# Delta rule and feed-forward on one core: the key products as 112-column products, the Gram products as 32-column ones

## The chip, the cores and the metric

The kernel runs on one core of a Trainium2 chip. The metric is the time of one execution on the device in microseconds (us). A run of a kernel is timed several times, and its median counts. One more execution is recorded instruction by instruction by the hardware profiler; all rows below come from that one.

The core has a matrix engine (PE, whose weight loads are listed apart as PEld), a vector engine (DVE), a scalar engine (ACT), GpSimd (POOL), and queues that start DMAs (SP here). Each engine works through its own instructions in a fixed order; an instruction whose input is late holds up everything behind it on that engine.

## The reference

Per head, a state of 48 x 48 is carried over 768 tokens. There are 4 x 8 = 32 heads. What the attention gives goes through two dense layers with a softplus between them.

```python
for t in range(S):
    kt, vt, bt = (k_n[:, :, t], v[:, :, t], beta[:, :, t, None])     # k_n: k over its norm
    y[:, :, t] = np.einsum('bhd,bhde->bhe', q[:, :, t], state)
    v_old = np.einsum('bhde,bhd->bhe', state, kt)
    state = state + bt[:, :, :, None] * np.einsum('bhd,bhe->bhde', kt, vt - v_old)
...
h = x @ w_in                                      # 3072 x 384 by 384 x 2048
g = np.maximum(h, 0.0) + np.log1p(np.exp(-np.abs(h)))
return (g @ w_out).astype(np.float32)
```

## The kernel before, in words

**Chunks.** The 768 tokens are cut into 12 chunks of 64 (`NS`, `C`). Within a chunk s the recurrence is solved with matrices: the Gram product K K^T of the chunk's keys (`gram`, L127) gives a triangular system, which is inverted (`invert`, on DVE, for two chunks at a time); `k_state` (L295) forms K S with the state S and takes it from the scaled values in `NV` (L299); `u_all` (L319) multiplies the inverse with them to U; `p_half` (L305) forms P, the products of keys and queries, and `mask_p` (L312) copies P under a triangular mask into the array `big`; `y_all` (L346) forms the outputs from the state, P and U; `state` (L331) makes the next state.

**Layout.** Heads go in 16 pairs, a head of a pair in each half of the 128 partitions. `big` has for each head 112 columns (`QW`): 64 for the queries or the masked P, then 48 for the state or U. `bv` and `be` are views of it, `be` sorted by the parity e of the pair. `tk[h]`, `dr[h]`, `lo[h]`, `hi[h]` are partition ranges: 64 tokens, the 48 feature rows in the opposite half, and the lower and upper 32 tokens. A product of 64 rows and 64 still columns occupies one quarter of PE's array, given by the half of its rows and the half of its output partitions. `quads` lists the 32 products of a step so that four neighbours take four different quarters; `k_state`, `gram` and `u_all` go by it. `p_half` uses two of the quarters only: rows in `dr[ab]`, outputs in `tk[ab]`. All these products are in fp32, and the trace has two matmul rows for each.

**Buffers.** Results of PE go to PSUM. The attention has four buffers there (`ps_a`, tile name `pa`), taken in turn; the dense layers have two for the first (`ps_h`, `ph`) and one for the second (`ps_o`, `po`). A product that needs a buffer waits until what stood in it has been read.

**What empties the Gram product.** ACT, in 12 copies per chunk: 8 of 32 partitions (L132) take the diagonal 32 x 32 blocks to `work`, 4 (L118) take the blocks below them to `off`.

**The dense layers** (`moe`) run beside the attention, chunk by chunk: L466 makes the hidden values, L470 to L472 on ACT and L474 to L477 on DVE make the softplus (and split it into a rounded part and a rest), L449 multiplies by the second weights. In the first chunk the weights are converted as well (L385 to L420).

**Order.** Up to the first chunk's state the order on PE, DVE, ACT and POOL is the order of the code (`manual_schedule`). From there on, generators for attention and dense layers yield pieces which `attend` and `target` mix, and the framework then settles the order of each engine when the program is built, with its own picture of time. PE works through pieces of both layers; the last tenth of the run is dense layers alone.

Chunks with an even number begin with `begin`: `cross_a` (L264), `arrange` and `cross_b` (L285, its result copied by ACT at L288) complete the inverses of two chunks. Even chunks 2, 4, 6 and 8 end with the Gram products of the two chunks after the next (`gram(s + 2)`, `gram(s + 3)`). The code of a chunk, around the change:

```python
k_state(s)
mask_p(0, p_half(s, 0))
yield
u_all(s)
...
mask_p(1, p_half(s, 1))
```

Of the kernel before, what the change touches and what calls it, by code (L numbers as in the profile page):

```python
# [7 lines left out]
F32 = mybir.dt.float32  # L8
# [4 lines left out]
ALU = mybir.AluOpType  # L13
# [4 lines left out]
B, H, S, D = 4, 8, 768, 48  # L18
NT, DM, DFF = B * S, H * D, 2048
P = 128  # L20
C = 64
HB = 32
# [13 lines left out]
def deltanet_moe(ctx, tc, kT, qT, kN, kI, vN, beta, wts, out):  # L36
# [33 lines left out]
    maskP = const.tile([P, C], F32, name="maskP")  # L70
    half = const.tile([P, 1], F32, name="half")
    bet = const.tile([P, NS, NP], F32, name="bet")
    W, HF, ST, OFF, TT, LTD, LDS, NN, NV, X = {}, {}, {}, {}, {}, {}, {}, {}, {}, {}

    copies = (nc.scalar.copy, nc.vector.tensor_copy)

# [25 lines left out]
    def parity(t):  # L102
        return t.rearrange("p (a e) c -> p e a c", e=2)
# [16 lines left out]
    def gram(s):  # L120
        if s not in OFF:
            OFF[s] = two.tile([P, NP, HB], F32, name="off", bufs=3)
        pas = [ps_a.tile([P, NP // 2, C], F32, name="pa") for e in range(2)]
        kt = kts[s % 3]
        for i, e, p, ab, t in quads:
            k = kt[dr[ab], p, :]
            nc.tensor.matmul(pas[e][tk[t], i, :], k, k, start=True, stop=True)  # L127
        u, j = divmod(s, 2)
        for e in range(2):
            for h in range(2):  # L130
                for rows, c in ((lo[h], 0), (hi[h], HB)):
                    nc.scalar.copy(parity(LTD[u][rows, j * NP:(j + 1) * NP])[:, e],  # L132
                                   pas[e][rows, :, c:c + HB])
        copy_below(s, pas)

    def gram_diagonal(s, pool, name):
        pas = [pool.tile([P, NP // 2, HB], F32, name=name) for e in range(2)]
# [150 lines left out]
            copies[s < 1 and h](tt[lo[h], :, HB:], pm[lo[h]])  # L288


    def k_state(s):

        pks = [ps_a.tile([P, NP // 2, D], F32, name="pa") for e in range(2)]
        for i, e, p, ab, t in quads:
            nc.tensor.matmul(pks[e][tk[t], i, :], kts[s % 3][dr[ab], p, :], bv[dr[ab], ab, p, C:],  # L295
                             start=True, stop=True)
        for e in range(2):
            r = parity(NV[s])[:, e]
            nc.vector.tensor_tensor(r, r, pks[e], op=ALU.subtract)  # L299

    def p_half(s, g, pool=None, name="pa"):
        pt = (pool or ps_a).tile([P, 8, C], F32, name=name)
# [213 lines left out]
    def chunk(s):  # L516
        more = s % 2 == 0 and 2 <= s < NS - 2
        if s % 2 == 0:
            load_v(s + 1)
            if more:  # L520
                load_k(s + 2)
                nm = norms(s // 2 + 1)
                next(nm)
            yield from begin(s)
        k_state(s)
        mask_p(0, p_half(s, 0))
        yield
        u_all(s)
        if s % 2 and s + 1 < NS:
            load_v(s + 1)  # L530
        mask_p(1, p_half(s, 1))
        if s % 2 == 0:
            cross_b(s + 1)
        if more:

            for _ in range(3):
                next(nm)
        yield
        last = y_all(s)
        if s + 1 < NS:  # L540
            with tc.issue_after(last[1].ins):
                scale_v(s + 1)
        yield
        if s + 1 < NS:
            state(s)
            load_ki(s + 1)
            if more:
                with tc.issue_after(last[0].ins):
                    next(nm)
                with tc.issue_after(last[1].ins):  # L550
                    next(nm)
            yield
        if more:
            u = s // 2 + 1
            systems(u)
            load_k(s + 3)
            gram(s + 2)
            cols[u] = run(nm)
            yield
            gram(s + 3)  # L560
            yield
            background.append(invert(u, *cols[u]))
# [105 lines left out]

    def attention():
        nonlocal steps_done  # L670
        k_state(1)
        mask_p(0, p_half(1, 0))
        yield
        u_all(1)
        mask_p(1, p_half(1, 1))
        yield
        last = y_all(1)
        with tc.issue_after(last[1].ins):
# [102 lines left out]
```

## Time and profile before

| what | value |
|---|---|
| time, median of 3 runs (range) | 681.18 us (679.97 to 684.1) |
| span of the profiled execution | 679.6 us |
| PE busy | 615.5 us, 91% |
| DVE busy | 453.6 us, 67% |
| ACT busy | 393.9 us, 58% |
| Gram products, L127 | 640 matmul rows; 80 copies L132 and 40 of the 48 copies L118 belong to them |
| K S, L295 | 704 matmul rows, 22 subtractions L299 |
| P, L305 into `pa` | 704 matmul rows, 44 maskings L312 |

[...]

### The profile page before, as it was taken

What the parts mean: (1) busy time and instruction counts of PE and PEld (TensorE: products, weight loads), DVE (VectorE), ACT (ScalarE), POOL (GpSimd) and SP (SyncE); (2) the same over time, 40 slices, a digit from 0 to 9 for tenths busy, and PEclk for the clock granted to TensorE, in tenths of its full rate; (3) what the DMA queues carried; (4) which work ended last, traced back from release to release, by engine and by line L of the source; (5) the groups of instructions that cost most, each with busy time, mean ns of one, the idle gap of its engine ahead of it and who ended that gap; (6) DMA issues with size and microseconds to landing.
All of it is one profiled execution on the core that took longest, in us unless ns stands there. A gap on an engine that the chain in (4) does not pass through costs nothing.

```text
span 679.6 us, 22869 instructions
## 1 busy us (share of the span) xinstructions
PE 615.5 (91%) x10096; PEld 573.8 (84%) x10096; DVE 453.6 (67%) x970; ACT 393.9 (58%) x747; POOL 30.4 (4%) x56
## 2 busy tenths in 40 slices
PE   4456977889987999989999999999989999999997
PEld 3346755679886999989999989998989999999997
DVE  4956499987456896556987538985547985544443
ACT  4344669789565447475456684554675555454433
POOL 3100010000000001000001000001000001000000
PEclk9998988999989999998999989996999999999999
DMA  9827284000140120140210322200401200200000
GB/s 226 273 92 201 71 269 134 1 25 4 50 106 25 48 60 25 49 106 26 66 41 27 81 73 72 61 24 3 106 2 49 60 24 4 60 14 25 1 24 23
DMA packets 35091, 44.73 MB, mean 66 GB/s; under 512 B 21776, under 2 KB 27184, under 8 KB 34992
## 3 DMA queue, kind: packets, MB, share of 16 engines
q1 hardware_dynamic: 34992, 43.27, 22.8%
q8 instruction: 79, 1.29, 0.8%
q14 instruction: 20, 0.16, 0.1%
HBM read 36.27 MB, written 4.72 MB: 60 GB/s over the span
## 4 chain that ended last, share of the span: by engine, by line
PE 65%; ACT 15%; DVE 11%; DMA 5%; issue 3%; SPq 1%; ACTq 0%; DVEq 0%
PE ph L466 26%; PE po L449 24%; PE pa L346 4%; PE pa L305 3%; ACT work L132 3%; DMA ka<-kN 3%; PE pa L319 2%; PE pa L285 2%; PE pa L331 2%; DMA w<-wts 2%; ACT off L118 2%; ACT a L472 2%; PE pa L295 1%; ACT a L471 1%; ACT tt L276 1%
## 5 line engine op out<-in xcount | busy, mean ns | idle before, releaser
L466 PE MATMUL ph<-x,w 128*128 128x256 f32 x1680 | 243.0, 296 | 4.3 <-DVE a L474 3.1
L466 PEld LDWEIGHTS ph<-x,w 128*128 128x128 f32 x1680 | 227.1, 195 | 11.8 <-DVE a L474 2.4
L449 PE MATMUL po<-w,gh 128*128 128x384 f32 x768 | 209.9, 359 | 6.7 <-DVE gh L480 6.0
L449 PEld LDWEIGHTS po<-w,gh 128*128 128x128 f32 x768 | 136.1, 191 | 17.8 <-DVE gh L480 7.6
L470 ACT ACTIVATE a<-ph 128x512 f32<-128x512 f32 x96 | 57.4, 598 | 161.3 <-PE ph L466 154.8
L474 DVE SCALAR_TENSOR_TENSOR a<-ph,a 128x512 f32<-128x512 f32 x88 | 60.6, 690 | 112.7 <-ACT a L472 112.5
L449 PE MATMUL po<-w,gl 128*128 128x384 f32 x352 | 119.8, 340 | 0.0
L449 PEld LDWEIGHTS po<-w,gl 128*128 128x128 f32 x352 | 66.7, 190 | 0.8 <-DVE gl L477 0.4
L477 DVE TENSOR_TENSOR gl<-a,gh 128x512 fp32r<-128x512 f32 x88 | 60.8, 691 | 3.2
L471 ACT ACTIVATE a<-a 128x512 f32<-128x512 f32 x96 | 60.7, 633 | 2.7
L472 ACT ACTIVATE a<-a 128x512 f32<-128x512 f32 x96 | 60.7, 632 | 2.3
L230 DVE TENSOR_TENSOR Z<-Z,work 128x84 f32<-128x84 f32 (+14 forms) x148 | 44.2, 305 | 2.9
L224 DVE TENSOR_TENSOR work<-Z,ltq 128x84 f32<-128x84 f32 (+14 forms) x148 | 44.1, 305 | 2.5
L476 DVE CAST gh<-a 128x512 fp32r<-128x512 f32 x88 | 37.6, 427 | 7.8 <-PE po L449 5.6
L312 DVE TENSOR_TENSOR big<-pa,maskP 64x512 f32<-64x512 f32 x44 | 30.2, 687 | 16.7 <-PE pa L305 16.2
L346 PEld LDWEIGHTS pa<-big 128*64 128x64 f32 x768 | 26.6, 147 | 8.9 <-ACT big L323 5.3
L346 PE MATMUL pa<-big 128*64 128x64 f32 x768 | 29.6, 234 | 4.7 <-ACT big L323 4.1
L323 ACT COPY big<-pa 64x384 f32<-64x384 f32 x46 | 21.6, 471 | 18.3 <-PE pa L319 17.5
L305 PE MATMUL pa<-big,kt 48*64 48x64 f32 x704 | 28.0, 235 | 4.2 <-ACT off L118 4.2
L278 POOL MEMSET tt<- 32x512 f32 x24 | 12.9, 537 | 410.6 <-PE pa L264 155.8
L132 ACT COPY work<-pa 32x256 f32<-32x256 f32 x80 | 28.9, 362 | 3.3 <-issue 2.4
L305 PEld LDWEIGHTS pa<-big,kt 48*64 48x64 f32 x704 | 25.4, 149 | 5.1 <-ACT off L118 4.6
(102 smaller groups left out, 648.7 us busy)
## 6 DMA issues: line engine op xcount, KB each, us to landing
w<-wts SPq DMA_DIRECT2D x16, 768.0 KB, 5.9
kt<-kT SPq DMA_DIRECT2D x24, 192.0 KB, 4.4
big<-qT SPq DMA_DIRECT2D x24, 192.0 KB, 3.9
nv<-vN SPq DMA_DIRECT2D x12, 384.0 KB, 4.5
ki<-kI SPq DMA_DIRECT2D x24, 192.0 KB, 3.7
out<-ex SPq DMA_DIRECT2D x24, 192.0 KB, 1.9
ka<-kN SPq DMA_DIRECT2D x8, 384.0 KB, 3.3
x<-x SPq DMA_DIRECT2D x66, 32.0 KB, 2.1
```

The source lines that it names most:

```text
L132: nc.scalar.copy(parity(LTD[u][rows, j * NP:(j + 1) * NP])[:, e], pas[e][rows, :, c:c + HB])
L224: nc.vector.tensor_tensor(tmp[:, a:a + r, 0:j], Z[:, a + j + 1:a + n, a + j:a + j + 1].to_broadcast([P, r, j]), lq[:, a + j:a + j + 1, a:a ...
L230: nc.vector.tensor_tensor(z, z, tmp[:, a:a + r, 0:j], op=ALU.add)
L305: nc.tensor.matmul(pt[tk[ab], i, :], kts[s % 3][dr[ab], 8 * g + i, :], bv[dr[ab], ab, 8 * g + i, 0:C], start=True, stop=True)
L346: nc.tensor.matmul(py[tk[ab], i, :], big[:, at + C:at + 2 * C], big[:, at:at + C], start=True, stop=True)
L449: nc.tensor.matmul(po[:, h, 0:DM], g[b][:, f - f0, h * P:(h + 1) * P], weight(f, a, DM, DM), start=(f == 0 and i == 0), stop=end)
L466: nc.tensor.matmul(ph[:, f - f0], weight(f, a, k * P, P), xr[b][k], start=(c == 0), stop=(c == len(terms1) * NK - 1))
L470: nc.scalar.activation(a, ph, AF.Abs)
L471: nc.scalar.activation(a, a, AF.Exp, scale=-1.0)
L472: nc.scalar.activation(a, a, AF.Ln, bias=1.0)
L474: nc.vector.scalar_tensor_tensor(a, ph, 0.0, a, op0=ALU.max, op1=ALU.add)
L477: softplus[0] = nc.vector.tensor_tensor(g[1], a, g[0], op=ALU.subtract)
```

## The change

`k_state` and the two calls of `p_half` per chunk become one function `keys(s, e)`: for each of 32 heads one product of the keys (still, 64 columns) with all 112 columns of `big`, which gives P and K S side by side. It goes by `quads`, so over four quarters. The results lie in four PSUM buffers per chunk (parity e, group g) where there were four before, two of K S and two of P. DVE takes K S from the values in four subtractions of 192 elements per partition (two of 384 before), and `mask_keys` masks P in eight instructions of 256 (four of 512 before). A buffer is free only when both its K S and its P have been read. All of P is now made ahead of `u_all`.

`gram` takes the 64 still columns in two halves of 32, each with the 64 moving columns, the upper half with the moving halves swapped. So the diagonal blocks of all four partition groups lie in the first 32 columns of the result and the blocks below them in the last 32 (the lower halves get the block above, which nothing reads). Four copies of 128 partitions empty it. The first chunk's own `gram_diagonal`, `gram_below` and `p_half` stay.

```diff
         for i, e, p, ab, t in quads:
-            k = kt[dr[ab], p, :]
-            nc.tensor.matmul(pas[e][tk[t], i, :], k, k, start=True, stop=True)
+            k = kts[s % 3][dr[ab], p, :]
+            for half, order in ((lo, k), (hi, k.rearrange("d (b c) -> d b c", b=2)[:, ::-1, :])):
+                first = half[0].start
+                nc.tensor.matmul(pas[e][half[t], i, :], k[:, first:first + HB], order,
+                                 start=True, stop=True)
         u, j = divmod(s, 2)
         for e in range(2):
-            for h in range(2):
-                for rows, c in ((lo[h], 0), (hi[h], HB)):
-                    nc.scalar.copy(parity(LTD[u][rows, j * NP:(j + 1) * NP])[:, e],
-                                   pas[e][rows, :, c:c + HB])
-        copy_below(s, pas)
+            nc.scalar.copy(parity(LTD[u][:, j * NP:(j + 1) * NP])[:, e], pas[e][:, :, 0:HB])
+        for e in range(2):
+            nc.scalar.copy(parity(OFF[s])[:, e], pas[e][:, :, HB:])
...
-    def k_state(s):
-
-        pks = [ps_a.tile([P, NP // 2, D], F32, name="pa") for e in range(2)]
-        for i, e, p, ab, t in quads:
-            nc.tensor.matmul(pks[e][tk[t], i, :], kts[s % 3][dr[ab], p, :], bv[dr[ab], ab, p, C:],
-                             start=True, stop=True)
-        for e in range(2):
-            r = parity(NV[s])[:, e]
-            nc.vector.tensor_tensor(r, r, pks[e], op=ALU.subtract)
+    def keys(s, e):
+
+        kt = kts[s % 3]
+        for g in range(2):
+            pk = ps_a.tile([P, 4, QW], F32, name="pa")
+            for i, f, p, ab, t in quads:
+                if f == e and i // 4 == g:
+                    nc.tensor.matmul(pk[tk[t], i % 4, :], kt[dr[ab], p, :], bv[dr[ab], ab, p, :],
+                                     start=True, stop=True)
+            r = parity(NV[s])[:, e, 4 * g:4 * g + 4]
+            nc.vector.tensor_tensor(r, r, pk[:, :, C:], op=ALU.subtract)
+            PK[s, e, g] = pk
+
+    def mask_keys(s, e):
+
+        for g in range(2):
+            pk = PK.pop((s, e, g))
+            for ab in range(2):
+                t = tk[ab ^ e]
+                nc.vector.tensor_tensor(
+                    be[tk[ab], ab, e, 4 * g:4 * g + 4, 0:C], pk[t, :, 0:C],
+                    maskP[t].unsqueeze(1).to_broadcast([C, 4, C]), op=ALU.mult)
...
-        k_state(s)
-        mask_p(0, p_half(s, 0))
+        for e in range(2):
+            keys(s, e)
+        for e in range(2):
+            mask_keys(s, e)
         yield
         u_all(s)
         if s % 2 and s + 1 < NS:
             load_v(s + 1)
-        mask_p(1, p_half(s, 1))
```

In the built program this stands as follows. Line numbers below `keys` are about 13 higher in the changed kernel: there L128 is the Gram product, L298 `keys`, L301 its subtraction, L310 the masking, L332 `u_all`, L359 `y_all`, L462 and L479 the dense layers, L483 to L490 the softplus. A row's `x` counts instructions of the program, of which the trace shows two each on PE.

PE at the end of chunk 4 and the start of chunk 5, before (`kt_74` and `kt_75` hold the keys of chunks 6 and 7, `kt_76` those of chunk 5):

```order
L127 MATMUL pa<-kt_74 64x64 x31
L127 MATMUL pa<-kt_75 64x64 x32
L466 MATMUL ph<-x_3989,w_1713 128x256 x9
L466 MATMUL ph<-x_3989,w_1718 128x256 x2
L295 MATMUL pa<-big,kt_76 64x48 x32
L305 MATMUL pa<-big,kt_76 64x64 x16
L466 MATMUL ph<-x_3989,w_1718 128x256 x7
```

and now:

```order
L128 MATMUL pa<-kt_74 32x64 x63
L128 MATMUL pa<-kt_75 32x64 x64
L298 MATMUL pa<-big,kt_76 64x112 x32
L479 MATMUL ph<-x_3981,w_1735 128x256 x9
L479 MATMUL ph<-x_3981,w_1740 128x256 x9
```

There are twice as many Gram products, the key products follow them at once, and the dense products that stood between come behind. On ACT at the same place, before:

```order
L472 ACTIVATE a<-a 128x512
L132 COPY work<-pa 32x8x32 x8
L118 COPY off<-pa 32x8x32 x4
L132 COPY work<-pa 32x8x32 x4
L118 COPY off<-pa 32x8x32 x2
L132 COPY work<-pa 32x8x32 x4
L118 COPY off<-pa 32x8x32 x2
L470 ACTIVATE a<-ph 128x512
```

and now:

```order
L485 ACTIVATE a<-a 128x512
L132 COPY work<-pa 128x8x32
L134 COPY off<-pa 128x8x32
L132 COPY work<-pa 128x8x32
L134 COPY off<-pa 128x8x32
L132 COPY work<-pa 128x8x32
L134 COPY off<-pa 128x8x32
L132 COPY work<-pa 128x8x32
L134 COPY off<-pa 128x8x32
L483 ACTIVATE a<-ph 128x512
```

Between the same neighbours stand 8 copies where 24 stood, and each buffer is done after two of them. At the start of chunk 10, PE before:

```order
L264 MATMUL pa<-tt,off 32x32 x64
L285 MATMUL pa<-off,tt 32x32
L295 MATMUL pa<-big,kt_75 64x48 x10
L285 MATMUL pa<-off,tt 32x32 x31
L295 MATMUL pa<-big,kt_75 64x48 x22
L305 MATMUL pa<-big,kt_75 64x64 x16
L319 MATMUL pa<-nv,tt 64x48 x32
L305 MATMUL pa<-big,kt_75 64x64 x16
L285 MATMUL pa<-off,tt 32x32 x32
L346 MATMUL pa<-big 64x64 x32
```

and now:

```order
L264 MATMUL pa<-tt,off 32x32 x64
L285 MATMUL pa<-off,tt 32x32
L298 MATMUL pa<-big,kt_75 64x112 x8
L479 MATMUL ph<-x_7367,w_2174 128x256
L462 MATMUL po<-w_2052,gh 128x384 x2
L285 MATMUL pa<-off,tt 32x32 x31
L298 MATMUL pa<-big,kt_75 64x112 x24
L332 MATMUL pa<-nv,tt 64x48 x32
L285 MATMUL pa<-off,tt 32x32 x32
L359 MATMUL pa<-big 64x64 x32
```

The products of U (L332) come right behind those of the keys, with none of P between. On DVE at the same place, before:

```order
L477 TENSOR_TENSOR gl<-a,gh 128x512
L299 TENSOR_TENSOR nv<-nv,pa 128x8x48 x2
L312 TENSOR_TENSOR big<-pa,maskP 64x8x64 x4
L354 TENSOR_TENSOR x_8087<-pa,x_8087 128x3x128
```

and now:

```order
L490 TENSOR_TENSOR gl<-a,gh 128x512
L301 TENSOR_TENSOR nv<-nv,pa 128x4x48
L310 TENSOR_TENSOR big<-pa,maskP 64x4x64 x2
L487 SCALAR_TENSOR_TENSOR a<-ph,a 128x512
L489 CAST gh<-a 128x512
L490 TENSOR_TENSOR gl<-a,gh 128x512
L301 TENSOR_TENSOR nv<-nv,pa 128x4x48
L310 TENSOR_TENSOR big<-pa,maskP 64x4x64 x2
L301 TENSOR_TENSOR nv<-nv,pa 128x4x48
L310 TENSOR_TENSOR big<-pa,maskP 64x4x64 x2
L301 TENSOR_TENSOR nv<-nv,pa 128x4x48
L310 TENSOR_TENSOR big<-pa,maskP 64x4x64 x2
```

The last subtraction, without which `u_all` isn't whole, stands behind six maskings, and here behind a softplus as well. On ACT the three ACTIVATEs of that softplus stand between the copies of `cross_a` and the two copies L288.

## Rows read from the trace of the kernel before

**Rows 1.** The page's busy time of each engine: us, share of the span, instructions.
```profile
PE 615.5 (91%) x10096; PEld 573.8 (84%) x10096; DVE 453.6 (67%) x970; ACT 393.9 (58%) x747; POOL 30.4 (4%) x56
```
**Rows 2.** Windows of 20 us: busy us by engine, granted clock, DMA share, GB/s.
```profile
100.00:120.00 20.00, 15.74 (x111) 11.05 (x107) 18.42 (x30) 19.70 (x38) 0.00 (x0) 0.91 0.51 140
...
300.00:320.00 20.00, 17.95 (x280) 16.90 (x273) 10.93 (x14) 15.27 (x36) 0.00 (x0) 0.83 0.13 41
...
400.00:420.00 20.00, 18.56 (x322) 17.08 (x322) 11.84 (x19) 14.04 (x33) 0.00 (x0) 0.91 0.06 21
420.00:440.00 20.00, 20.00 (x257) 19.31 (x254) 18.75 (x48) 10.38 (x21) 0.00 (x0) 1.00 0.37 91
```
**Rows 3.** Timeline of PE, odd chunks' start: start us, us, instructions, [idle before, releaser].
```profile
207.01 1.15 PE L305 MATMUL pa<-big,kt 48*64 48x64 f32 x32 [1.91 <-ACT off L118]
304.30 0.43 PE L295 MATMUL pa<-big,kt 48*64 48x48 f32 x6 [1.40 <-ACT off L118]
305.06 1.94 PE L295 MATMUL pa<-big,kt 48*64 48x48 f32 x58 [0.34 <-ACT off L118]
402.34 0.32 PE L295 MATMUL pa<-big,kt 48*64 48x48 f32 x4 [0.99 <-ACT off L118]
403.10 1.20 PE L295 MATMUL pa<-big,kt 48*64 48x48 f32 x60 [0.45 <-ACT off L118]
506.36 1.93 PE L305 MATMUL pa<-big,kt 48*64 48x64 f32 x32 [1.96 <-ACT off L118]
```
**Rows 4.** Timeline of ACT behind the Gram products of chunk 6.
```profile
300.52 2.97 ACT L132 COPY work<-pa 32x256 f32<-32x256 f32 x8
303.50 1.50 ACT L118 COPY off<-pa 32x256 f32<-32x256 f32 x4
```
**Rows 5.** Timeline of PE around chunk 7: blocks of fp32 products at full clock.
```profile
400.18 1.16 PE L127 MATMUL pa<-kt 48*64 48x64 f32 x64
408.34 1.15 PE L305 MATMUL pa<-big,kt 48*64 48x64 f32 x32
427.10 2.09 PE L346 MATMUL pa<-big 128*64 128x64 f32 x64
433.55 1.64 PE L331 MATMUL pa<-big,ki 128*48 128x48 f32 x64
```
**Rows 6.** Groups by line: shapes, count | busy us, mean ns | idle before, releasers.
```profile
L477 DVE TENSOR_TENSOR gl<-a,gh 128x512 fp32r<-128x512 f32 x88 | 60.8, 691 | 3.2
L471 ACT ACTIVATE a<-a 128x512 f32<-128x512 f32 x96 | 60.7, 633 | 2.7
L476 DVE CAST gh<-a 128x512 fp32r<-128x512 f32 x88 | 37.6, 427 | 7.8 <-PE po L449 5.6
L312 DVE TENSOR_TENSOR big<-pa,maskP 64x512 f32<-64x512 f32 x44 | 30.2, 687 | 16.7 <-PE pa L305 16.2
L299 DVE TENSOR_TENSOR nv<-nv,pa 128x384 f32<-128x384 f32 x22 | 11.2, 546 | 17.3 <-PE pa L295 17.3
L113 ACT COPY work<-pa 128x256 f32<-128x256 f32 x4 | 1.3, 370 | 1.5 <-PE pa L141 1.5
```
**Rows 7.** Timeline of all engines at the start of chunk 10.
```profile
568.52 0.59 ACT L270 ACTIVATE off<-pa 32x512 f32<-32x512 f32 x1
...
571.15 1.51 PE L319 MATMUL pa<-nv,tt 64*64 64x48 f32 x64
```
**Rows 8.** Timeline of all engines at the start of chunk 2.
```profile
175.52 1.02 PE L295 MATMUL pa<-big,kt 48*64 48x48 f32 x54 [0.54 <-issue]
...
177.21 1.01 DVE L299 TENSOR_TENSOR nv<-nv,pa 128x384 f32<-128x384 f32 x2
...
179.46 0.56 PE L319 MATMUL pa<-nv,tt 64*64 64x48 f32 x23 [0.40 <-issue]
```
**Rows 9.** Timeline of all engines behind the Gram product of chunk 2.
```profile
34.10 0.72 PE L247 MATMUL pa<-tt,x 32*32 32x16 f32 x36 [3.69 <-issue]
...
37.10 0.37 ACT L249 COPY x<-pa 128x256 f32<-128x256 f32 x1
```

More of the change, by code (lines that the diff above doesn't have):

```diff
@@ L72, in deltanet_moe @@
     bet = const.tile([P, NS, NP], F32, name="bet")
-    W, HF, ST, OFF, TT, LTD, LDS, NN, NV, X = {}, {}, {}, {}, {}, {}, {}, {}, {}, {}
+    W, HF, ST, OFF, TT, LTD, LDS, NN, NV, X, PK = {}, {}, {}, {}, {}, {}, {}, {}, {}, {}, {}
     copies = (nc.scalar.copy, nc.vector.tensor_copy)
@@ L123, in gram @@
         pas = [ps_a.tile([P, NP // 2, C], F32, name="pa") for e in range(2)]
-        kt = kts[s % 3]
         for i, e, p, ab, t in quads:
-            k = kt[dr[ab], p, :]
-            nc.tensor.matmul(pas[e][tk[t], i, :], k, k, start=True, stop=True)
+            k = kts[s % 3][dr[ab], p, :]
[3 more added lines that the diff above has]
+                                 start=True, stop=True)
         u, j = divmod(s, 2)
         for e in range(2):
-            for h in range(2):
-                for rows, c in ((lo[h], 0), (hi[h], HB)):
-                    nc.scalar.copy(parity(LTD[u][rows, j * NP:(j + 1) * NP])[:, e],
-                                   pas[e][rows, :, c:c + HB])
-        copy_below(s, pas)
+            nc.scalar.copy(parity(LTD[u][:, j * NP:(j + 1) * NP])[:, e], pas[e][:, :, 0:HB])
+        for e in range(2):
+            nc.scalar.copy(parity(OFF[s])[:, e], pas[e][:, :, HB:])
     def gram_diagonal(s, pool, name):
@@ L670, in attention @@
         nonlocal steps_done
-        k_state(1)
-        mask_p(0, p_half(1, 0))
+        for e in range(2):
+            keys(1, e)
+        for e in range(2):
+            mask_keys(1, e)
         yield
         u_all(1)
-        mask_p(1, p_half(1, 1))
         yield
```

## The prediction

> **What bounds the kernel now.** I read the page's busy times first, then windows of 20 us, then the timeline of PE where it idles, and last ACT and DVE at the same places. PE is busy 91% of the span, DVE 67%, ACT 58% [rows 1]. The windows show where the rest lies. The first 140 us are bound by loads and by the conversion of the weights on ACT and DVE: ACT works 19.70 of 20 us in the sixth window. From about 220 us on PE works 18 to 20 us of every 20, so that what PE no longer does there is won, as long as DVE keeps up: behind the start of chunk 7 DVE works 18.75 of 20 us [rows 2].
>
> In this stretch PE waits almost only at one kind of place, where an odd chunk's key products follow the Gram products that end an even chunk. The four buffers then hold Gram results, and ACT empties them with 24 copies. The waits are 1.91 us in chunk 3, 1.40 and 0.34 in chunk 5, 0.99 and 0.45 in chunk 7, 1.96 in chunk 9, in all 7.05 us, each ended by L118, the last of a buffer's copies [rows 3]. Behind such waits the granted clock falls to its lower level: the windows around chunks 5 and 7 have 0.83 and 0.91 on average [rows 2], and 58 products of K S take 1.94 us in chunk 5 where 60 take 1.20 in chunk 7 [rows 3].
>
> **The key products.** K S takes 60 products in 1.20 us [rows 3], so 1.28 for 64; P takes 1.15 for its first 32 [rows 5] and as much for the others. That is 3.6 us; blocks overlap their neighbours by about 0.1, so I count 3.3. The new block has 64 products on four quarters. A turn of four takes 1.16 / 16 = 0.072 us with 64 moving columns [rows 5]. For 48 more columns I take the price per column from L346 and L331, which go two at a time: (2.09 - 1.64) / 32 turns / 16 columns = 0.88 ns, though there the still columns grow along [rows 5]. So 0.072 + 48 x 0.00088 = 0.114 us a turn, 1.83 us for 16, and 1.5 us are saved per chunk. From below: 48 and 64 columns take nearly the same time a turn on four quarters (1.28 and 1.16 us per 64 products), so the further ones could be free, and 2.1 us saved. From above: were only two quarters at work at a time, 3.7 us, and 0.4 lost. I take 1.5, since there are far more columns than the 64 that a turn has been seen to hide. It counts in chunks 4, 6 and 8 in full (4.5 us); in 3, 5, 7, 9 and 11 at 1.2, since DVE is nearly full behind them (6.0 us); in chunk 1, which DVE and ACT bound, not at all. Together 10.5 us.
>
> **DVE's part.** By L299 and L312 an element costs (687 - 546) / 128 = 1.1 ns [rows 6]. The new subtraction of 192 takes 0.34 us, the masking of 256 takes 0.41; per chunk 4 x 0.34 + 8 x 0.41 = 4.6 us where it was 2 x 0.55 + 4 x 0.69 = 3.8. The 0.8 us more are hidden by PE's dense work where a piece of it follows.
>
> **The new wait.** `u_all` needs all four subtractions, and the last stands behind three others and six maskings: 4 x 0.34 + 6 x 0.41 = 3.8 us on DVE, with PE's key products done after 1.8. In most chunks dense products stand between. In chunks 2 and 10 none do, and queued behind `u_all` on PE are `cross_b` and the dense products. Chunk 2: DVE starts its subtractions at 177.21 [rows 8] and would reach the end of the last at 181.0; the second half of the U products takes 0.6 more, so U ends at 181.6 where it ended at 179.46 + 0.56 = 180.02 [rows 8]. The second half of P (1.1 us) no longer follows, which leaves +0.5. Chunk 10: ACT ends the `cross_a` copies at 569.11 [rows 7], then has three ACTIVATEs of about 0.63 ahead of L288 [rows 6], until 571.0; DVE's softplus takes two passes of 0.69 and a cast of 0.43 [rows 6], until 572.8; three subtractions and four maskings follow, until 575.5, and U ends at 576.1 where it ended at 571.15 + 1.51 = 572.66 [rows 7]. That is 3.4, less 0.5 for dense products pulled ahead: +2.9. Each leaves PE idle for some 3 us, and I count one fall of the clock as in chunk 7's window, (1 - 0.91) x 20 = 1.8 us [rows 2]. Together +5.2.
>
> **The Gram products.** PE gets 128 rows of 32 still and 64 moving columns in place of 64. If all eight pieces of the array (two row halves by four output groups) go at once, a Gram product stays at 16 turns, 1.16 us [rows 5]; if four go at a time it takes 32 turns, 2.3 us, +1.2; if two, as P does now (32 products in 1.15 us), 64 turns, 4.6 us, +3.4. Every block in rows 5 has as many at work as it has distinct pieces: P's two give 36 ns per product, the four of L127 18. I take +0.2 for each of the 8 Gram products behind 180 us: +1.6. Also, PE's instructions come in blocks, and in dense stretches PE waits for the next: between the waits of 0.54 and 0.40 us in chunk 2 lie 3.9 us [rows 8]. More Gram products make this worse and fewer key products better; I set it to nothing, within a us either way per pair of Gram products.
>
> **The copies.** One copy of 256 elements takes 0.37 us with 32 partitions (2.97 / 8) [rows 4] and with 128 (370 ns) [rows 6]. So a pair of Gram products costs ACT 3.0 us instead of 9.0, and the 7.05 us of waits shrink. I leave 1 us each in chunks 3 and 5, where the key products follow the second Gram product at once and their second half needs its buffers, and 0.4 in chunk 7: 4.6 us won, of 0 to 7.05. The clock lost (1 - 0.83) x 20 = 3.4 us and 1.8 us in the windows of chunks 5 and 7 [rows 2]; of this, and of chunk 9's, I take 3.5 back, of 0 to 7. In the sixth window, which ACT fills [rows 2], chunk 3's copies shrink by 8 x 0.37 = 3.0 us and DVE gains 0.8: -2.0. In the start, chunk 2's copies shrink by as much, but L249, which begins at 37.10, also needs products that PE ran only from 34.10 on, after 3.69 us without instructions [rows 9], and 64 more products stand ahead of them: -1.0, of 0 to 1.5.
>
> **The sum.** -10.5 + 5.2 + 1.6 - 4.6 - 3.5 - 2.0 - 1.0 = -14.8 us. The profiled execution spans 679.6 us, 1.6 below the median of 681.18; 679.6 - 14.8 + 1.6 = 666.4 us.
>
> [...]
>
> **The rivals.** First, the Gram products go four at a time: 8 x (1.2 - 0.2) = 8 us more, 674.4. For it: no row shows eight pieces at once. Chance 0.18.
>
> Second, two at a time: 8 x (3.4 - 0.2) = 25.6 us more, 692. This is the case slower than before. It decides from 8 x 2.0 on, that is once a Gram product costs some 2 us more than now. For it: consecutive products share their rows; against: four quarters already share rows in pairs. Chance 0.07.
>
> Third, DVE's longer run before U is not hidden in chunks 4, 6 and 8 either. Each then loses its 1.5 and PE waits 3.8 - 1.8 = 2.0 with a fall of the clock of 1.8: 3 x 3.5 to 5.3, say 12 us more, 678. For it: the softplus stands among the maskings on DVE there too; against: dense products stand between on PE. Chance 0.15.
>
> Fourth, it goes better: further columns are free (0.6 more in 8 chunks, 5 us) and the clock never falls at odd chunks (3.5 more): 658. Chance 0.12.
>
> **How the numbers follow.** The forecast has chance 0.48, with a range of its own of 661 to 673. A measurement of this kernel can tell about 1% from no change, so faster means below 674.4 and slower above 688.0. Faster: nearly all of the forecast (0.46), the fourth rival, and half of the first (0.10): 0.68. Slower: the second rival and a little for mishaps of the order: 0.08. Between: 0.24. The range of 657 to 679 takes in the fourth, first and third rivals.
>
> **What would show it.** Right: the rows L298 take 1.7 to 2.0 us per 64 where nothing holds them; L128 takes 1.1 to 1.5 us per 128; the idle times of PE ended by the Gram copies sum to under 3 us; the granted clock is 1.00 around chunks 7 and 9; PE idles 2 to 4 us ahead of L332 in chunk 10. Wrong: L128 at over 2 us per 128, PE idle before L332 in chunks 4, 6 and 8, or the dense products' softplus late behind the block of maskings in odd chunks.

## The result, and the profile after

The changed kernel takes 674.73 us (median of 19 runs) against 681.18: a ratio of 0.9898, with an interval of 0.9874 to 0.9922. It is 6.9 us faster by this ratio, 1.0%, where 14.8 us were forecast. The ratio leaves out runs in which the core was in a slower state; the medians of all runs differ by 6.45 us. The profiled execution of the changed kernel spans 671.1 us, 8.5 less than before.

The page's busy times, the windows that answer to [rows 2], and the groups of the lines concerned:

```profile
PE 611.4 (91%) x10032; PEld 570.8 (85%) x10032; DVE 462.2 (69%) x1036; ACT 362.1 (54%) x667; POOL 30.4 (5%) x56
```

```profile
100.00:120.00 20.00, 15.20 (x62) 11.12 (x51) 19.90 (x31) 15.34 (x26) 0.00 (x0) 0.83 0.65 189
300.00:320.00 20.00, 19.83 (x248) 19.09 (x249) 16.26 (x35) 7.59 (x16) 0.00 (x0) 1.00 0.14 42
400.00:420.00 20.00, 20.00 (x237) 18.71 (x236) 17.49 (x39) 10.72 (x21) 0.00 (x0) 1.00 0.14 49
```

```profile
L298 PE MATMUL pa<-big,kt 48*64 48x112 f32 x704 | 39.3, 284 | 0.0
L128 PE MATMUL pa<-kt 48*32 48x64 f32 x1280 | 16.9, 234 | 8.9 <-issue 8.2 <-ACT big L347 0.7
L134 ACT COPY off<-pa 128x256 f32<-128x256 f32 x20 | 7.7, 390 | 0.0
L132 ACT COPY work<-pa 128x256 f32<-128x256 f32 x20 | 7.4, 376 | 5.8 <-PE pa L128 5.7
L310 DVE TENSOR_TENSOR big<-pa,maskP 64x256 f32<-64x256 f32 x88 | 37.0, 420 | 1.4
L301 DVE TENSOR_TENSOR nv<-nv,pa 128x192 f32<-128x192 f32 x44 | 15.3, 352 | 19.1 <-PE pa L298 18.3
```

ACT works 32 us less, its windows at chunks 5 and 7 are half empty, and the clock there is 1.00. No Gram copy ends a wait of PE any more. PE's timeline shows what came instead (start, us, instructions, [idle before, releaser]). Where the releaser is `issue`, the trace shows no semaphore that PE waited for; I call these waits for instructions, and the experiments on the supply of instructions give the figures behind the name.

```profile
199.63 0.81 PE L128 MATMUL pa<-kt 48*32 48x64 f32 x59 [3.00 <-issue]
200.38 5.56 PE L298 MATMUL pa<-big,kt 48*64 48x112 f32 x64
...
300.17 0.63 PE L128 MATMUL pa<-kt 48*32 48x64 f32 x38 [2.31 <-issue]
...
389.85 1.49 PE L128 MATMUL pa<-kt 48*32 48x64 f32 x128
...
393.55 1.73 PE L128 MATMUL pa<-kt 48*32 48x64 f32 x128
395.21 2.96 PE L298 MATMUL pa<-big,kt 48*64 48x112 f32 x64
398.10 2.16 PE L479 MATMUL ph<-x,w 128*128 128x256 f32 x16
...
562.45 0.67 PE L332 MATMUL pa<-nv,tt 64*64 64x48 f32 x22 [1.57 <-DVE nv L301]
563.73 0.67 PE L332 MATMUL pa<-nv,tt 64*64 64x48 f32 x28 [0.61 <-DVE nv L301]
```

A Gram product of 128 rows takes 1.49 us, 0.33 more than the 64 rows before [rows 5]; the one of 1.73 us has a gap of 0.25 in it. The key products take 2.96 us, not 1.83, and 2.89 up to the start of the next block. Inside two pairs of Gram products PE waits for instructions, and in chunk 10 for the subtractions.

To see where time went, I use the first dense product (L479, before L466). Its 1,680 rows come in the same order in every kernel, and where nothing but dense products runs their distances agree to 0.1 us. The table, worked out from the single records of the traces, gives the time between the starts of rows number 0, 144, 216, 312, 504, 600, 960, 1080, 1200, 1344 and 1679 of each trace, less the same before. "2>3" is the stretch from the end of chunk 2 into chunk 3; the last column holds the half-clock loss, (1 - granted clock) x span, as mean over all runs of the kernel with its standard error. The granted clock is the share of PE's full clock that the profile shows; in the traces of the two kernels it is 1.0 or 0.5 at any time (0.50 from 200.5 to 207.1 us in the changed kernel). The 10.5 us behind the last row are equal in all and left out, but for the sum.

| kernel | start | 1 | 2 | 2>3 | 4 | 4>5 | 6, 6>7 | 8 | 8>9 | 10 | 11 | sum | half clock |
|---|---|---|---|---|---|---|---|---|---|---|---|---|---|
| before (us) | 65.3 | 82.5 | 36.4 | 43.5 | 62.2 | 39.7 | 116.3 | 47.7 | 44.6 | 48.4 | 82.6 | 679.6 | 25.1 (0.4) |
| changed | +1.7 | -3.8 | +1.2 | -4.0 | +0.9 | -3.0 | -2.5 | -0.1 | -2.5 | +3.6 | -0.1 | -8.5 | 23.4 (0.7) |
| e1 keys alone | -0.6 | +4.8 | +4.1 | -0.2 | -0.7 | +1.9 | -1.7 | -3.6 | -1.7 | +4.4 | -0.1 | +6.8 | 28.7 (2.0) |
| e8 (e2) Gram alone | +1.2 | -0.1 | +0.3 | -3.2 | +1.7 | +0.5 | -4.3 | -4.4 | -3.1 | +1.8 | 0.0 | -9.6 | 26.8 (1.2) |
| e3 four quarters | +0.9 | -2.9 | +3.2 | -4.0 | +0.5 | -0.2 | -3.5 | +1.0 | -3.7 | +4.0 | -1.0 | -5.8 | 30.1 (2.4) |
| e5 subtractions first | +2.3 | -1.0 | -1.7 | +0.3 | +1.2 | -0.6 | -2.9 | +2.3 | -2.5 | +1.2 | +0.1 | -1.2 | 26.2 (1.1) |
| e7 both | +2.3 | -0.4 | -1.5 | -0.3 | +0.8 | -1.3 | -4.4 | +0.7 | -3.7 | +0.6 | -1.2 | -8.5 | 27.9 (0.9) |
| e9 both, from chunk 2 | +1.5 | -2.4 | -4.7 | +2.3 | +0.6 | -2.7 | -3.5 | -3.1 | -3.7 | +0.3 | -0.1 | -15.5 | 23.3 (1.9) |
| e10 Gram spread | +1.6 | +2.7 | -2.6 | -8.3 | +0.9 | -2.8 | +8.1 | -6.0 | -1.7 | -0.5 | -1.2 | -9.8 | 18.5 (1.0) |

Chunk 8's swing between +2 and -6 is one fall of the clock, there or not: before, it lay at 466 to 476 us. Each row of the table is one execution (that of e9 is the fastest of its six), so a difference of a few us between two rows can be chance; medians decide.

### The profile page after: what moved, and what is told of

Same layout as the page of the kernel before. It is cut to its first block, busy times and chain, and to the rows that moved or that the text cites. A ratio compares the mean times of both kernels' runs of the same rounds, so it can differ in the third digit from the quotient of the medians.

```text
span 671.1 us, 22732 instructions
## 1 busy us (share of the span) xinstructions
PE 611.4 (91%) x10032; PEld 570.8 (85%) x10032; DVE 462.2 (69%) x1036; ACT 362.1 (54%) x667; POOL 30.4 (5%) x56
## 3 DMA queue, kind: packets, MB, share of 16 engines
q8 instruction: 79, 1.29, 0.8%
## 4 chain that ended last, share of the span: by engine, by line
PE 77%; DVE 8%; issue 6%; ACT 6%; DMA 2%; SPq 1%; DVEq 0%; ACTq 0%
PE ph L479 28%; PE po L462 28%; PE pa L298 4%; PE pa L359 4%; PE pa L344 2%; PE pa L128 2%; PE pa L285 2%; PE pa L332 2%; PE pa L264 1%; DVE big L310 1%; PE pa L254 1%; ACT tt L276 1%; DMA ka<-kN 1%; DVE tt L237 1%; DMA kt<-kT 1%
## 5 line engine op out<-in xcount | busy, mean ns | idle before, releaser
L479 PE MATMUL ph<-x,w 128*128 128x256 f32 x1680 | 240.5, 294 | 6.1 <-ACT w L423 4.3
L479 PEld LDWEIGHTS ph<-x,w 128*128 128x128 f32 x1680 | 224.0, 192 | 14.7 <-ACT w L423 5.0
L462 PE MATMUL po<-w,gh 128*128 128x384 f32 x768 | 207.0, 355 | 2.1 <-DVE gh L493 1.6
L483 ACT ACTIVATE a<-ph 128x512 f32<-128x512 f32 x96 | 57.4, 598 | 167.7 <-PE ph L479 164.4
L462 PEld LDWEIGHTS po<-w,gh 128*128 128x128 f32 x768 | 134.9, 190 | 12.0 <-DVE gh L493 2.4
L487 DVE SCALAR_TENSOR_TENSOR a<-ph,a 128x512 f32<-128x512 f32 x88 | 60.5, 689 | 107.0 <-ACT a L485 105.9
L462 PE MATMUL po<-w,gl 128*128 128x384 f32 x352 | 119.5, 340 | 0.0
L462 PEld LDWEIGHTS po<-w,gl 128*128 128x128 f32 x352 | 66.5, 189 | 0.6 <-DVE gl L490 0.2
L490 DVE TENSOR_TENSOR gl<-a,gh 128x512 fp32r<-128x512 f32 x88 | 60.8, 691 | 3.3 <-DVE Z L230 0.2
L298 PE MATMUL pa<-big,kt 48*64 48x112 f32 x704 | 39.3, 284 | 0.0
L310 DVE TENSOR_TENSOR big<-pa,maskP 64x256 f32<-64x256 f32 x88 | 37.0, 420 | 1.4
L298 PEld LDWEIGHTS pa<-big,kt 48*64 48x64 f32 x704 | 35.2, 148 | 1.7 <-issue 0.8
L359 PEld LDWEIGHTS pa<-big 128*64 128x64 f32 x768 | 28.9, 154 | 5.4 <-ACT big L336 2.0
L359 PE MATMUL pa<-big 128*64 128x64 f32 x768 | 32.0, 243 | 1.5 <-ACT big L336 1.2
L301 DVE TENSOR_TENSOR nv<-nv,pa 128x192 f32<-128x192 f32 x44 | 15.3, 352 | 19.1 <-PE pa L298 18.3
```

The lines of the kernel that those rows point to most:

```text
L298: nc.tensor.matmul(pk[tk[t], i % 4, :], kt[dr[ab], p, :], bv[dr[ab], ab, p, :], start=True, stop=True)
L310: nc.vector.tensor_tensor(be[tk[ab], ab, e, 4 * g:4 * g + 4, 0:C], pk[t, :, 0:C], maskP[t].unsqueeze(1).to_broadcast([C, 4, C]), op=ALU.mult)
L359: nc.tensor.matmul(py[tk[ab], i, :], big[:, at + C:at + 2 * C], big[:, at:at + C], start=True, stop=True)
L462: nc.tensor.matmul(po[:, h, 0:DM], g[b][:, f - f0, h * P:(h + 1) * P], weight(f, a, DM, DM), start=(f == 0 and i == 0), stop=end)
L479: nc.tensor.matmul(ph[:, f - f0], weight(f, a, k * P, P), xr[b][k], start=(c == 0), stop=(c == len(terms1) * NK - 1))
L483: nc.scalar.activation(a, ph, AF.Abs)
```

## The experiments

My theory: the key products run on two quarters at a time, so all the gain comes from the Gram copies. Its rival: the key products gained as forecast and something else took it back.

**e1, e2, e8: each half alone.** e1 takes the old `gram` into the changed kernel; e2 and e8 are one kernel, the new `gram` in the kernel before.

```diff
 e1 (changed kernel)
-            for half, order in ((lo, k), (hi, k.rearrange(...)[:, ::-1, :])):
-                nc.tensor.matmul(pas[e][half[t], i, :], k[:, first:first + HB], order, ...)
+            nc.tensor.matmul(pas[e][tk[t], i, :], k, k, start=True, stop=True)
 ... (and the 12 copies of 32 partitions)
```

> Only the joint key products with their subtractions and maskings; the Gram products and their 24 copies per pair stay as in the kernel before. Theory (the key products run on two quarters at a time, so they hardly gain): L298-like blocks of 64 take 2.8 to 3.0 us against 3.3 before, some 0.4 us in 8 chunks = -3 us; the wait ahead of U costs 3.6 us in chunk 10 and about 1 in chunk 2; the waits behind the Gram copies stay: 680 to 684 us against 681, no change that can be told. Rival (the key products do bring most of the gain and the Gram part takes it back): 676 us or less.

> Only the Gram products of 32 still columns with their 4 copies; K S and P stay two blocks as in the kernel before. Theory (the whole gain comes from the copies): the waits of PE that Gram copies end go from 7.05 us to under 1, the clock falls behind them go too, of which the supply of instructions takes some back: 671 to 676 us. Rival (the Gram part takes time, the key part wins): 679 us or more.

> The Gram part alone once more, for a profile that can be compared stretch by stretch. Theory (its gain of 6.6 us is waits behind copies and falls of the clock that go, less waits for instructions): no wait of PE is ended by a Gram copy from 200 us on, waits for instructions within Gram products of 2 to 6 us in chunks 2 and 4, K S and P at 1.2 us for 64 and 1.15 for 32 as before. Rival (the gain comes in the start, where ACT is full): by 200 us it is ahead by 5 us or more, and little comes behind.

Measured: e1 690.26 us, ratio 1.0165 (1.0103 to 1.0227), slower than either expected; e2 674.34 us, 0.9897 (0.9865 to 0.9930); e8, one run, 671.69 us. e2's trace is of an execution of 2,195 us and is not used here; e8 stands for it. The Gram part alone gives all of the gain, and the key products on top of it nothing. The rival falls. In e8 no Gram copy ends a wait of PE, and the waits for instructions within Gram products are 2.0 us from 140 us on (PE's waits: us in total, times, longest):

```profile
PE pa L128 <- issue: 2.0, 2, 1.7
```

That e1 lost 9 us neither theory had. In the table it loses most in chunks 1, 2 and 10. Its timelines of DVE and PE in chunk 1 show what happens there:

```profile
84.48 0.35 DVE L301 TENSOR_TENSOR nv<-nv,pa 128x192 f32<-128x192 f32 x1
84.87 0.86 DVE L310 TENSOR_TENSOR big<-pa,maskP 64x256 f32<-64x256 f32 x2
...
89.11 0.90 DVE L420 SCALAR_TENSOR_TENSOR ex<-w,ex 128x768 int32<-128x768 int32 x1
...
90.27 0.31 DVE L301 TENSOR_TENSOR nv<-nv,pa 128x192 f32<-128x192 f32 x1
```

```profile
90.64 1.09 PE L332 MATMUL pa<-nv,tt 64*64 64x48 f32 x24 [4.79 <-DVE nv L301]
```

Of the four subtractions the rows show the third and the last. The last stands behind a round of the weight conversion (L410 to L420) and instructions of the norms. U needs all four, and PE waits 4.79 us. I had counted chunk 1 at nothing. In the changed kernel the same wait is 1.4 us.

**e3: four quarters.** Both parities' tiles are open at once.

```diff
-    def keys(s, e):
+    def keys(s):
...
-            pk = ps_a.tile([P, 4, QW], F32, name="pa")
-            for i, f, p, ab, t in quads:
-                if f == e and i // 4 == g:
-                    nc.tensor.matmul(pk[tk[t], i % 4, :], ...)
+            pks = [ps_a.tile([P, 4, QW], F32, name="pa") for e in range(2)]
+            for i, e, p, ab, t in quads:
+                if i // 4 == g:
+                    nc.tensor.matmul(pks[e][tk[t], i % 4, :], ...)
```

> The changed kernel, with the key products of both parities alternating, so that four quarters can be at work; same number of products, subtractions and maskings. Theory (two quarters at a time is what failed of the forecast): 64 products take 1.6 to 1.9 us in place of 2.89, 1.0 us less in 8 chunks and a little in the others: 665 to 668 us against 674.7. Rival one (the 112 moving columns, not the quarters, set the turn, as on one shared path into the array): the block stays at 2.7 to 2.9 us and the time at 674 +- 2. Rival two (the block shortens but U then waits for DVE's subtractions): the block falls, PE idles ahead of U in more chunks, 671 to 675 us.

Measured: 674.06 us, 0.9884 (0.9826 to 0.9942). PE's timeline in chunk 4, at chunk 9 and at chunk 10, and two windows of it (the changed kernel's clock is 1.00 at 300 to 320); U is L333 here, the masking L311 and the subtraction L302:

```profile
302.57 0.77 PE L128 MATMUL pa<-kt 48*32 48x64 f32 x39 [3.30 <-issue]
...
498.75 1.76 PE L298 MATMUL pa<-big,kt 48*64 48x112 f32 x64
...
565.43 0.91 PE L333 MATMUL pa<-nv,tt 64*64 64x48 f32 x32 [1.72 <-DVE big L311]
566.88 1.09 PE L333 MATMUL pa<-nv,tt 64*64 64x48 f32 x28 [0.54 <-DVE nv L302]
```

```profile
300.00:320.00 20.00, 17.43 (x210) 16.61 (x211) 12.15 (x23) 7.54 (x15) 0.00 (x0) 0.83 0.15 42
460.00:480.00 20.00, 19.67 (x352) 18.25 (x349) 9.03 (x21) 8.16 (x17) 0.00 (x0) 0.66 0.24 62
```

The block takes 1.76 us at chunks 9 and 11, so the theory on the quarters holds for the block and its first rival falls. In the trace's single records two rows start together every 96 ns in the changed kernel and four every 95 ns here. In chunks 2, 6 and 7 the block has a gap of 0.37 to 0.74 us in it, and in chunks 3 and 5 it ran at the lower clock and took 3.26. But the time stayed: 665 to 668 us were expected of the theory, and the second rival, by which U then waits for DVE, has the time that was measured. Where dense products follow (chunks 9, 11, "8>9" and "11" in the table) about 1.1 us are won. Where U follows (chunks 2 and 10), DVE sets U's start and nothing is won. And the half-clock loss rises from 23.4 to 30.1 us. In chunk 4 PE waits 3.30 us for instructions in place of 2.31, with half clock behind it from 302.9 to 309.7 us. Why the loss rises as a whole is not shown.

**e5, e7, e9: the subtractions first.** e5 is the changed kernel with this edit, e7 is e3 with it, e9 is e7 but for chunk 1.

```diff
+        with tc.issue_after(PK[s].ins):          # PK[s]: the chunk's last subtraction
             for e in range(2):
                 mask_keys(s, e)
```

> The changed kernel, with all eight maskings of a chunk queued on DVE behind its four subtractions; PE's work is the same. Theory (U waits for the last subtraction behind six maskings, and that is what chunks 2 and 10 lose): the wait of PE for the subtraction in chunk 10 goes from 1.57 + 0.61 us to under 1 us in all, or dense products take its place, the half clock from 565.6 to 569.0 goes with it, and chunk 2 gains some 1 us: 669 to 672 us against 674.7. Rival (the softplus ahead on DVE or the copies of the other operand set U's start): the same waits, 674 +- 2 us.

> Four quarters for the key products (as in the run on four quarters) and all subtractions ahead of the maskings together. Theory (what four quarters save is lost in the wait for U and in the clock behind it): each alone gives little, both together give the 1.2 us in most chunks: 664 to 668 us against 674.7 and 674.1. Rival (the saved time goes into waits for instructions and falls of the clock at the Gram products): 671 to 675 us.

> As the run with four quarters and the subtractions first, but chunk 1 keeps the maskings between the subtractions. In that run and in the one with the subtractions first alone, chunk 1 took 2.5 to 2.8 us more, since PE's products of U then wait for the maskings to give their buffers free. Theory: chunk 1 is back to 3 us less than before (where it is -0.4), and the time falls by about 2.5 us from 673.8, to 670 to 672. Rival (chunk 1's time hangs on the place of the softplus on DVE, not on the maskings): 673 to 676 us.

Measured: e5 680.32 us, 0.9998 (0.9966 to 1.0031); e7 673.76, 0.9885 (0.9850 to 0.9920); e9 674.19, 0.9862 (0.9810 to 0.9914), its six runs between 665.83 and 675.11. e5's timeline of PE, in chunk 1 and in chunk 10:

```profile
89.83 2.31 PE L332 MATMUL pa<-nv,tt 64*64 64x48 f32 x64 [2.51 <-DVE big L310]
...
573.83 1.15 PE L332 MATMUL pa<-nv,tt 64*64 64x48 f32 x64
```

In chunk 10 the wait and the fall of the clock are gone and 2.4 us are won, as the theory had it. But U also needs two of the four buffers, which the maskings now give free later, so chunk 1 loses 2.8 us. Chunk 8 loses 2.4 by a longer fall of the clock (463.4 to 477.1 us, in the changed kernel 456.4 to 466.6). Of the 4.3 us lost in "2>3", where chunk 2 wins 2.9, and of the 2.4 in "4>5" the cause is not shown. As a whole my expectation for e5 was wrong, the rival's unchanged 674 us too: it is 1% slower than the changed kernel. e7's time is the one that its rival named (671 to 675 us). Sparing chunk 1 (e9) brought 2 us there in the profile and nothing that the medians tell.

**e4, e6, e10, e11, e12: the supply of instructions.** e4 moves the first Gram product of a pair ahead, behind the output products. e6 issues 64 rows a Gram product in place of 128; it leaves out the swapped moving halves, so that the blocks of the upper rows lie at other columns and its numbers are not the reference's. e10 is e9 with Gram products in four pieces, released into the next chunk, and with four steps of the inversion at a time in place of two; e11 and e12 do this in chunk 2 alone, in the changed kernel and in e9.

```diff
 e6
-            for half, order in ((lo, k), (hi, ...)):
-                nc.tensor.matmul(pas[e][half[t], i, :], k[:, first:first + HB], order, ...)
+            nc.tensor.matmul(pas[e][tk[t], i, :], k, k, start=True, stop=True)
 e10
+        for n, (i, e, p, ab, t) in enumerate(quads):
+            if n and n % (32 // parts) == 0:
+                yield "part"
...
+        if more:
+            steps_done = s + 1               # behind y_all
```

> The changed kernel, with the first Gram product of a pair moved ahead to stand behind the output products of its chunk, so that dense products stand between the two; nothing else changes. Theory (a run of more than some 256 small products outruns the supply of instructions): PE's waits for instructions of 3.0 us in chunk 2 and 2.3 in chunk 4 go, and with the first also the half clock from 200.4 to 207.2 us, which costs another 2 to 3: 668 to 671 us against 674.7. Rival (as many instructions must be fetched anyway, so the waits only show at another place): waits for instructions of the same sum elsewhere, 674 +- 2 us.

> The changed kernel, with the Gram products again as 32 products of 64 still columns each, but emptied by the 4 full copies: the upper 32 rows' blocks come out at wrong columns, so that the inverses and all behind them are computed from wrong numbers; the work and its order stay. It tells what the doubled number of Gram products costs. Theory (the doubled number costs 0.3 us a Gram product and, above all, waits for instructions, with a fall of the clock): the waits of 3.0 us in chunk 2 and 2.3 in chunk 4 shrink to under 2.5 in all, 5 to 7 us less than the changed kernel: 668 to 670 us. Rival (the waits for instructions come from the whole run of small products and stay, or move): 673 to 675 us.

> As the run before it in this list (four quarters, subtractions first from chunk 2 on), with each Gram product issued in four pieces of 16 products, and with the last steps of an even chunk (state, Gram products) released into the next chunk, so that 6 to 30 dense products stand between the pieces; the inversion may take four steps a group in place of two. Theory (the waits for instructions, 4.4 to 6.1 us in the runs so far, and the falls of the clock behind them at 200 and 303 us come from the unbroken run of state, Gram and key products): no wait for instructions over 0.5 us from 190 us on but those of the start, no half clock in chunks 3 and 5, and 4 to 7 us less than the run before it: 664 to 668 us. Rival (the Gram products end later, so the inversion ends later, and the next even chunk's steps are pushed together with waits of their own): the waits move to the starts of chunks 4, 6 and 8, 671 to 678 us.

> The changed kernel (key products on two quarters, maskings between the subtractions), with the Gram products of chunk 2 alone issued in four pieces each and released into the next chunk, so that 12 to 30 dense products stand between the pieces; the inversion behind them may take four steps a group. All other Gram products stay. Theory (the wait for instructions of 3.00 us and the half clock from 200.4 to 207.2 come from the unbroken run there): both go, and from the start of chunk 2 to chunk 3 it takes 4 to 6 us less than the changed kernel; some of it is given back at the start of chunk 4, where the inversion ends later and U follows the key products at once: 669 to 672 us against 674.7. Rival (the later inversion costs as much as is won): 673 to 677 us.

> All that has shown a gain in its own stretch together: four quarters, the subtractions first from chunk 2 on, and the Gram products of chunk 2 spread. Theory (the gains are in different stretches and add up: 4 to 6 us of the spread on the 674.2 of the run without it): 667 to 670 us, under both kernels. Rival (a fall of the clock comes at another place instead): 672 to 675 us, with the granted clock no higher than 0.962 on average.

Measured: e4 679.28 us, 0.9979 (0.9944 to 1.0014); e6 671.18, 0.9845 (0.9813 to 0.9876); e10 674.46, 0.9895 (0.9853 to 0.9938); e11 677.50, 0.9920 (0.9883 to 0.9957); e12 675.89, 0.9896 (0.9856 to 0.9936). The waits of PE for instructions between 186 and 320 us, 5.3 in the changed kernel, are 0.8 in e4, none in e6 and none in e10. PE's waits in the changed kernel and then in e4:

```profile
PE pa L128 <- issue: 5.3, 2, 3.0
```

```profile
PE pa L128 <- issue: 0.8, 1, 0.8
```

So they do come from the doubled number of Gram rows in an unbroken run. In chunk 2 of e6 a wait for ACT stands at the same place and could hide one; in chunk 4 nothing holds PE there, and the wait is gone. That PE waits for its instructions I read from the packets of a queue that the page calls `instruction` (q8, 79 packets, 1.29 MB): in the traces of the kernels before and after, each of the 15 such waits of over 1 us ends 1.26 to 1.62 us behind the end of one. In the changed kernel the last packets ahead of the two waits end at 198.31 and 298.75 us, and PE goes on at 199.63 and 300.17. Without these waits and without the 0.33 us a product e6 is 3.5 us faster than the changed kernel. e4 is 0.8% slower than it, since in e4 and e6 another wait took their place. ACT in e6, then PE in e6, then ACT and PE in e4 (L156 and L159 are the square of the keys for the norms, L344 a copy of the state, L126 the Gram product, L487 a part of the softplus):

```profile
200.90 0.84 ACT L156 ACTIVATE ka<-ka 128x768 f32<-128x768 f32 x1 [4.83 <-DMA ka<-kN]
```

```profile
203.30 0.48 PE L126 MATMUL pa<-kt 48*64 48x64 f32 x4 [4.89 <-ACT big L344]
```

```profile
390.80 0.85 ACT L159 ACTIVATE ka<-ka 128x768 f32<-128x768 f32 x1 [4.26 <-DMA ka<-kN]
```

```profile
393.28 0.73 PE L479 MATMUL ph<-x,w 128*128 128x256 f32 x4 [2.03 <-DVE a L487]
```

ACT stands at the square, whose load is queued on SP behind the six writes of x; copies or the softplus stand behind the square. In the changed kernel this wait is 1.8 to 2.2 us long and mostly hidden. e10 shows the theory whole in its stretch: 8.3 us less in "2>3", no half clock there. But the inversion for chunk 6 ends later, at 364.0 us where it is 356.2 in the changed kernel, and the 8.1 us lost in chunk 6 are the rival. e11 repeats it on a smaller scale: 7.8 us less than before in "2>3", and 4.6 more in chunk 4. e12, which was to add up the gains of e9 and e11 to 667 to 670 us, does not: its 675.89 us lie between them.

**e13, e14, e15: the load for the square at the chunk's start,** in the changed kernel, in e9 and in the kernel before.

```diff
-        for j in range(2):
-            ka = kas[j] if kas else load_ka(2 * u + j)
+        loaded = kas or [load_ka(2 * u + j) for j in range(2)]
+        for j in range(2):
+            ka = loaded[j]
```

> The changed kernel, with the second load of k for the norms started at the chunk's start (into the inversion's free tile) in place of behind the six writes of x on SP's queue. Nothing else changes on PE. In the runs so far ACT stands 1 to 6 us at the square of this load, and the Gram or state copies queue behind it. Theory (this wait on ACT, whose length hangs on the order on SP, is what takes gains back at chunks 3, 5 and 7): ACT's idle time ahead of L162-like squares (2.16, 2.23, 1.78 us) goes; with Gram products emptied at once PE gains 1 to 3 us: 671 to 674 us against 674.7. Rival (in this kernel ACT is early enough everywhere, PE's waits there are for instructions): unchanged, 673 to 676 us.

> Four quarters, the subtractions first from chunk 2 on, and the early load. Without the early load this kernel took 674.2 us, with a wait of PE of 4.47 us for Gram copies that stood behind the square's 5.85 us on ACT. Theory (that wait takes back what four quarters and the order of the subtractions win): it goes, and the time is 667 to 670 us. Rival (the clock falls instead wherever a wait is gone, since the falls come from the small products themselves): 672 to 675 us with a mean granted clock of 0.96 or less.

> The kernel before with the early load alone. Theory: PE's 2.0 us ahead of the second Gram product in chunk 2 stand behind the square's load and go; the other waits of the Gram copies stay: 677 to 680 us against 681. Rival (copies of the Gram products set all of it): 680 to 682 us.

Measured: e13 673.29 us, 0.9902 (0.9866 to 0.9938); e14 670.31, 0.9825 (0.9785 to 0.9865); e15 683.84, 1.0033 (1.0004 to 1.0062). e14 is the fastest kernel here, under the changed kernel and e13, but its interval overlaps that of e9, and e13 and e15 show no gain of the load's own. In e14 ACT still waits in chunk 2, and PE behind it (L164 is the square, L303 the key products, L138 a Gram copy):

```profile
200.17 0.84 ACT L164 ACTIVATE ka<-ka 128x768 f32<-128x768 f32 x1 [3.86 <-DMA ka<-kN]
```

```profile
201.60 2.31 PE L303 MATMUL pa<-big,kt 48*64 48x112 f32 x32 [2.20 <-ACT off L138]
```

ACT's wait is gone in chunk 6 and shorter in chunk 4 (0.94 us in e14, 1.64 in e9). In chunk 2 it is 3.86 us in e14, where it is 5.85 in e9, and 3.09 in e13, where it is 2.16 in the changed kernel. So the edit settles nothing about chunk 2. In e5, e7 and e9 as well PE waits there for Gram copies that stand behind this square, 1.2, 2.0 and 4.5 us. How much of e14's gain is the load, and how much that its runs lost 21.9 us at half clock where those of e9 lost 23.3, stays open.

## Why the prediction went wrong in size

**Key products: wrong, the step that failed.** "The new block has 64 products on four quarters." They go through one parity at a time (`f == e`), and with the parity fixed, `ab ^ e` ties the rows half to the columns half: two quarters are ever at work. I read the sequence as that of `quads` and did not follow the filter. My own upper bound, two quarters, was the case: 2.96 us (I had bounded it at 3.7). The term of -10.5 us should have been 8 x (3.3 - 2.89) = -3.3, and the waits for U take more than that: chunks 2 and 10 lose 1.2 and 3.6 us in the table. With both terms (-10.5 + 5.2) the key products were to bring 5.3 us; on top of the Gram part they bring nothing (674.73 against 674.34 in e2). The size of a turn of four was nearly right: 0.095 us by e3 for 0.114.

**That "what PE no longer does there is won": wrong as well.** Four quarters alone would not have brought the forecast. In e3 the block takes 1.76 us where nothing holds it, as the prediction had it, and the time is 674.06 us, not 666.4. Against the changed kernel the saving came through at chunks 9 and 11; around chunk 5 a longer wait for instructions and a fall of the clock took 2.8 us, and over the runs the half-clock loss is 6.7 us higher. So a share of 91% did not make PE's time the kernel's time.

**Supply of instructions: wrong.** I set it to nothing "within a us either way per pair"; in two of four pairs it costs 3.0 and 2.3 us, and a fall of the clock from 200.4 to 207.2 us (before, one from 199.2 to 202.7 stood there). A third wait for instructions of 1.96 us, at 160.9 us, was not there before either. By e6 the supply and the longer Gram products together cost some 3.5 us, where 1.6 were counted.

**Copies: right, and better; clock: right in place.** The waits of 7.05 us [rows 3] went whole where I left 2.4. At 300 and 400 us the clock is 1.00, but as mean over the runs the half-clock loss fell by 1.7 us only, from 25.1 to 23.4; my terms, 3.5 back and 1.8 lost to a new fall, come to the same. There was a wait I had not seen, 2.12 us of PE for the softplus in chunk 3 of the trace before, which went too:

```profile
219.51 0.43 PE L466 MATMUL ph<-x,w 128*128 128x256 f32 x1 [2.12 <-DVE a L474]
```

**Gram products: right.** 0.33 us each for 0.2; the first and second rivals fall. That the first had named the time (674.4) is luck: its reason, four products at a time, is not what happened. The second had 4.6 us for 128 rows going two at a time; the measured 1.49 us decides against it here.

**The new wait: right for chunk 10,** +3.6 us in the table for +2.9 and a fall of the clock; chunk 2 has +1.2 for +0.5. The third rival, the same in chunks 4, 6 and 8, did not come.

**Start: wrong.** It is 1.7 us slower, not 1.0 faster. The doubled Gram rows of chunk 2 stand in it too: PE's waits for instructions there sum to 22.4 us, where they are 17.7 before and 17.3 in e6. The stretch behind it, which the sixth window stands for, won 3.8 for 2.0.

Of the signs named, L128 at 1.49 us, no idle time by Gram copies, the clock at chunks 7 and 9, and 2.18 us ahead of L332 in chunk 10 came as said; L298 did not.

## What to carry to other kernels

Before a block is costed as running on all quarters of the array, write down rows half and columns half of four consecutive products: the loop here filtered on the one that links them, and 64 rows took 2.96 us on two quarters where they take 1.76 on four. With PE 91% busy and its rest made of short waits, the faster block paid here only where the next work was ready: the same 1.1 us were won before dense products and not before U. Count instructions as well as time: doubling 128 short rows to 256 in one run cost more here in waits for instructions (5.3 us) than in the rows themselves (8 x 0.33).

## What was not expected of the hardware

A turn of rows, those that start together, took as long here with two quarters as with four: 96 ns (the changed kernel) and 95 ns (e3) with 112 moving columns, 58 ns with 64 (P, and the old Gram products). So two more quarters cost no time here. With 48 moving columns the old K S took 58 ns a turn of four, and L331, the state in the kernel before, 45 ns a turn of two; what makes the difference is not shown.

As I read it, more than four rows of 32 still columns went at a time: 128 rows took 1.49 us, where 32 turns of four would take 1.86 at 58 ns. In the records of the block at 389.85 us the first 32 rows start in groups of eight, the later ones one by one.

That PE's instructions come in blocks is my reading of three things in the traces. The changed kernel has 79 packets of 16 KB on the queue q8 `instruction` for 2 x 10,032 rows of PE and PEld, in the mean 254 rows to a packet, and the 128 rows of a Gram product, with a load for each, make 256 in 1.49 us. No semaphore ends the waits called `issue`, and a packet's end stands 1.26 to 1.62 us ahead of the end of each of the 15 over 1 us. And from 186 to 320 us these waits go when the rows are fewer (e6) or spread (e10): 5.3 us in the changed kernel, none there.

The time at half clock differs from run to run of one kernel: e9's six runs lie between granted clocks of 0.960 and 0.977, and between 675 and 666 us. Within a kernel, over the runs of all of them, 1 us more of half-clock loss goes with 0.5 us more of span.
